# Fused linear attention and SwiGLU kernel: value loads released by the first key, first weight slices 256 columns wide

## The chip, the cores and the metric

One core of one Trainium2 chip runs the whole program. The metric is the device time of one execution in microseconds. Lower is better. Times are medians of several executions on the chip. Every profile is one execution; its span (first to last recorded instruction) is about 2 us shorter than its device time. In this document PE is TensorE, ACT is ScalarE, DVE is VectorE, POOL is GpSimd and SP is the sync engine; POOL and SP issue the DMA loads.

## The reference, cut to what matters

Eight batches, eight heads, 576 tokens, head size 64; then a SwiGLU layer over the 4608 tokens, 512 to 1536 to 512.

```python
q_s = softmax(q, axis=-1)                       # over the head size
k_s = softmax(k, axis=2)                        # over the tokens
kv  = einsum('bhsd,bhse->bhde', k_s, v)
x   = einsum('bhsd,bhde->bhse', q_s, kv)        # then transposed to [tokens, 512]
g   = x @ w_gate
out = (g * sigmoid(g) * (x @ w_val)) @ w_out    # float32
```

## The kernel before

The attention of batch 0 comes first, a chain of short steps that wait for each other. Then PE runs one long stream: the FFN of batch 0 in 12 units (m = 0 to 11, one unit per 128 columns of d_ff), the output products of batch 0 with the attention of batch 1 between them, the FFN of batch 1, and so on.

Queries and keys of batch 0 are loaded by SP. The values of batch 0, and all weights, are loaded by POOL, with DMAs that also cast float32 to bfloat16. POOL issues in program order, so whatever it waits for at the first value load delays every weight behind it:

```python
for G in range(NG):                       # NG = 2 groups of 4 heads
    qd = load("q", q, 0, G)               # SP
    load("k", k, 0, G)
d = nc.gpsimd.dma_start(out=v16[0], in_=head_ap(v, 0, 0))      # POOL, casts
tc.add_manual_dep(d.ins, qd.ins.name, SYNC, reason="order of loads")
for t0, t1 in BANKS:
    nc.gpsimd.dma_start(out=v16[1][:, :, 64*t0:64*t1], in_=head_ap(v, 0, 1, t0, t1))
# ... memsets, exp of q and k, sums ...
for c0, n in ((0, 128), (128, 256), (384, 384), (768, 384), (1152, 384)):
    w_slice(wg, moe_w_gate, c0, n)        # POOL, casts
    w_slice(wv, moe_w_val, c0, n)
w_dma = [wo_slice(m0, 3) for m0 in (0, 3, 6, 9)]
# ... attention of batch 0 ...
load_batch(1, w_dma[-3], by_group=True)   # SP: loads of batch 1 after the 2nd w_out slice
for m in range(MT):
    m_unit(0, S, m, by_part=(m == 0))     # g_ps (wg) and u_ps (wv) of columns 128 m ...
```

After the 12 units come `o_mm(0)`, `o_mm(1)` (output products, o_ps), then the transposes of batch 1's queries (tp), its kv and x products, `o_mm(2)`, `o_mm(3)`, and the FFN of batch 1's first 448 tokens (the g_ps matmuls of 128x448).

The softmax here doesn't subtract the row's maximum and nothing guards it: scores larger than these inputs give would overflow.

Of the kernel before, what the change touches and what calls it, by code (L numbers as in the profile page):

```python
# [11 lines left out]
SYNC = mybir.DependencyInfo(mybir.DependencyClass.Sync, mybir.DependencyReason.DATA)  # L12
# [3 lines left out]
def kernel(  # L16
# [48 lines left out]
    def head_ap(src, b, G, t0=0, t1=T):  # L65
        return bass.AP(
            tensor=src.tensor,
            offset=src[b, 4 * G].offset + 64 * t0,
            ap=[[T * 64, 128], [2 * HSTR, 2], [1, (t1 - t0) * 64]],
        )  # L70

    def load(what, src, b, G, pieces=((0, T),), after=None):
        t_ = ld.tile([128, 2, T * 64], FP32, tag=what, name=what)
        raw[what, b, G] = t_
        last = None
        for t0, t1 in pieces:
            last = nc.sync.dma_start(out=t_[:, :, 64 * t0:64 * t1], in_=head_ap(src, b, G, t0, t1))  # L77
            if after is not None:
                tc.add_manual_dep(last.ins, after.ins.name, SYNC, reason="order of loads")
                after = None  # L80
        return last
# [11 lines left out]
    def w_slice(dst, src, c0, n):  # L93
        ap = bass.AP(
            tensor=src.tensor,
            offset=src[0, c0].offset,
            ap=[[d_ff, 128], [128 * d_ff, KT], [1, n]],
        )
        return nc.gpsimd.dma_start(out=dst[:, :, c0:c0 + n], in_=ap)  # L99
# [251 lines left out]

    make_identity(nc, ident)
    with tc.manual_schedule():
        for G in range(NG):
            qd = load("q", q, 0, G)
            load("k", k, 0, G)
        d = nc.gpsimd.dma_start(out=v16[0], in_=head_ap(v, 0, 0))
        tc.add_manual_dep(d.ins, qd.ins.name, SYNC, reason="order of loads")
        for t0, t1 in BANKS:
            nc.gpsimd.dma_start(out=v16[1][:, :, 64 * t0:64 * t1], in_=head_ap(v, 0, 1, t0, t1))  # L360

# [14 lines left out]
        norm_mul(0, 0, BANKS)  # L376
        norm_sum(0, 1, BANKS)

        for c0, n in ((0, 128), (128, 256), (384, 384), (768, 384), (1152, 384)):
            w_slice(wg, moe_w_gate, c0, n)  # L380
            w_slice(wv, moe_w_val, c0, n)
        w_dma = [wo_slice(m0, 3) for m0 in (0, 3, 6, 9)]
# [199 lines left out]
```

## Time and profile before

| | before |
|---|---|
| device time, median of the first 3 runs | 320.3 us (320.14 to 320.42) |
| span of the profiled run | 318.2 us |
| PE busy | 305.4 us, 96% |
| value load issued by POOL | 8.31 us |
| first kv matmul | 12.45 us |
| first g_ps matmul | 15.81 us |
| first output product (12 FFN units done) | 41.19 us |
| loads of batch 1 start | 35.91 us |

From the page of the kernel before: the span, the busy time of each engine (microseconds, share, number of instructions), and the chain of waits that ended last, by engine and by line.

```profile
span 318.2 us, 4858 instructions
PE 305.4 (96%) x1865; PEld 152.1 (48%) x1894; DVE 163.2 (51%) x277; ACT 147.5 (46%) x218; POOL 29.5 (9%) x37
...
PE 79%; DMA 12%; DVE 3%; POOL 1%; ACT 1%; issue 1%; SPq 1%; DVEq 0%
PE g_ps L298 25%; PE u_ps L298 25%; PE o_ps L322 24%; DMA wo<-in_moe_w_out_dram 5%; DMA q<-in_q_dram 5%; DMA wv<-in_moe_w_val_dram 2%; PE kv L191 2%; DVE rs L138 1%; PE xp L267 1%; DVE qs L152 1%; PE o_ps L342 1%; ACT eq L124 1%; SPq L77 1%
```

PE is busy 96% of the span, but 12% of the chain is DMA. The timeline of the kernel before shows where. Columns: start in us, busy us, engine, line, operation, output<-inputs, shapes, count, and in brackets the idle time before it and what ended it.

```profile
8.04 1.26 ACT L124 ACTIVATE eq<-q 128x640 bf16<-128x640 f32 x2 [0.68 <-DMA q<-in_q_dram]
8.31 0.86 POOL L357 DMA_DIRECT2D v<-in_v_dram  x1 [7.01 <-DMA q<-in_q_dram]
...
12.45 0.68 PE L410 MATMUL kv<-v,ek 64*128 64x128 bf16 x18 [1.08 <-DMA v<-in_v_dram]
...
15.81 0.90 PE L298 MATMUL g_ps<-xt,wg 128*128 128x320 bf16 x4
...
19.15 1.15 PE L298 MATMUL g_ps<-xt,wg 128*128 128x320 bf16 x8 [1.02 <-DMA wg<-in_moe_w_gate_dram]
...
20.60 1.15 PE L298 MATMUL u_ps<-xt,wv 128*128 128x320 bf16 x8 [0.30 <-DMA wv<-in_moe_w_val_dram]
20.84 0.77 POOL L107 DMA_DIRECT2D wo<-in_moe_w_out_dram  x1 [0.71 <-DMA wv<-in_moe_w_val_dram]
...
41.19 5.34 PE L322 MATMUL o_ps<-wo,hr 128*128 128x512 bf16 x23
...
45.82 1.16 ACT L124 ACTIVATE eq<-q 128x1152 bf16<-128x1152 f32 x1 [1.28 <-DMA q<-in_q_dram]
...
46.76 0.68 PE L166 MATMUL tp<-ident,qs 128*128 128x128 bf16 x9 [0.23 <-DVE qs L152]
```

The reader is to see three DMA waits of PE in the first 21 us (1.08, 1.02 and 0.30 us), a value load that POOL issues only when the second query has landed, and a second place that waits for DMA: at 45.82 us ACT starts the exponential of batch 1's second query, 1.28 us after it was free, when that query has landed. The chain of waits in order of time (start, duration, what):

```profile
12.80 7.75 DMA wv<-in_moe_w_val_dram
...
20.84 15.06 DMA wo<-in_moe_w_out_dram
...
37.42 8.37 DMA q<-in_q_dram
...
45.82 1.17 ACT eq L124
```

### The profile page before, as it was taken

The numbers are of one execution on the slowest core, as the hardware profiler recorded it, in microseconds if no ns is written. First come the engines' busy times: TensorE is split into PE (matmuls) and PEld (weight loads), VectorE is DVE, ScalarE is ACT, GpSimd is POOL, SyncE is SP. The second block draws the span as 40 slices with busy tenths as digits, with TensorE's granted clock in tenths as the row PEclk, the third lists the DMA queues.
The fourth block names the chain that finished last, engine by engine and source line by source line (L and its number), as shares of the span: only waits on it lengthen the run. The fifth ranks groups of instructions, "written<-read, shape, count | busy, mean of one in ns | idle before, by whom it ended". The sixth has DMA issues, their size and how long they took to land.

```text
span 318.2 us, 4858 instructions
## 1 busy us (share of the span) xinstructions
PE 305.4 (96%) x1865; PEld 152.1 (48%) x1894; DVE 163.2 (51%) x277; ACT 147.5 (46%) x218; POOL 29.5 (9%) x37
## 2 busy tenths in 40 slices
PE   6789999999999999999999999999999999999994
PEld 2457854454445444544444444444444444444443
DVE  3634467595663558354936393548454333423421
ACT  4653378824654474547374556445734022312300
POOL 0950011200200020002000200020000000000000
PEclk9999999999999999999999999999999999999999
DMA  7999999459164907391539453854320202020124
GB/s 280 134 190 203 239 399 390 158 90 383 61 129 99 387 28 143 70 377 66 118 66 311 158 105 70 270 211 84 69 55 0 55 13 66 0 68 1 33 68 101
DMA packets 40360, 45.75 MB, mean 144 GB/s; under 512 B 17424, under 2 KB 24080, under 8 KB 40336
## 3 DMA queue, kind: packets, MB, share of 16 engines
q1 hardware_dynamic: 32480, 39.99, 41.9%
q0 software_dynamic: 7696, 5.31, 11.5%
q8 instruction: 15, 0.25, 0.3%
q10 hardware_dynamic: 160, 0.13, 0.2%
q14 instruction: 9, 0.07, 0.1%
HBM read 37.75 MB, written 9.44 MB: 148 GB/s over the span
## 4 chain that ended last, share of the span: by engine, by line
PE 79%; DMA 12%; DVE 3%; POOL 1%; ACT 1%; issue 1%; SPq 1%; DVEq 0%
PE g_ps L298 25%; PE u_ps L298 25%; PE o_ps L322 24%; DMA wo<-in_moe_w_out_dram 5%; DMA q<-in_q_dram 5%; DMA wv<-in_moe_w_val_dram 2%; PE kv L191 2%; DVE rs L138 1%; PE xp L267 1%; DVE qs L152 1%; PE o_ps L342 1%; ACT eq L124 1%; SPq L77 1%; POOL wg L99 0%; POOL v L360 0%
## 5 line engine op out<-in xcount | busy, mean ns | idle before, releaser
L305 ACT ACTIVATE sg<-g_ps 128x512 bf16<-128x512 f32 (+2 forms) x120 | 65.0, 554 | 140.2 <-PE g_ps L298 120.6
L306 DVE TENSOR_TENSOR hr<-sg,u_ps 128x512 bf16<-128x512 bf16 (+2 forms) x120 | 74.4, 629 | 88.8 <-PE u_ps L298 81.4
L298 PE MATMUL g_ps<-xt,wg 128*128 128x512 bf16 (+2 forms) x469 | 110.0, 357 | 2.0 <-DMA wg<-in_moe_w_gate_dram 1.0
L298 PE MATMUL u_ps<-xt,wv 128*128 128x512 bf16 (+2 forms) x468 | 109.7, 357 | 0.9 <-DMA wv<-in_moe_w_val_dram 0.3
L322 PE MATMUL o_ps<-wo,hr 128*128 128x512 bf16 x414 | 93.0, 379 | 0.4 <-issue 0.2
L298 PEld LDWEIGHTS <-wv 128*128 128x128 bf16 x480 | 46.9, 98 | 46.9 <-DMA wv<-in_moe_w_val_dram 0.6
L298 PEld LDWEIGHTS <-wg 128*128 128x128 bf16 x480 | 45.7, 98 | 46.5 <-DMA wg<-in_moe_w_gate_dram 1.3
L322 PEld LDWEIGHTS <-hr 128*128 128x128 bf16 x420 | 40.9, 98 | 49.1
L113 DVE COPY o_sb<-o_ps 128x512 f32<-128x512 f32 x33 | 22.4, 680 | 39.2 <-PE o_ps L322 37.3
L127 POOL CAST vb<-v 128x1152 bf16<-128x1152 f32 x14 | 16.0, 1146 | 173.3 <-DMA v<-in_v_dram 173.0
L138 DVE TENSOR_REDUCE rs<-eq 128x18 f32<-128x1152 bf16 (+2 forms) x18 | 21.7, 1214 | 13.1 <-ACT eq L124 13.0
L152 DVE TENSOR_TENSOR qs<-eq,rr 128x1152 bf16<-128x1152 bf16 (+2 forms) x18 | 22.2, 1245 | 0.1
L124 ACT ACTIVATE eq<-q 128x1152 bf16<-128x1152 f32 (+2 forms) x18 | 18.1, 1050 | 4.5 <-DMA q<-in_q_dram 4.5
L124 ACT ACTIVATE ek<-k 128x1152 bf16<-128x1152 f32 x16 | 18.0, 1158 | 0.3 <-DMA k<-in_k_dram 0.2
L305 ACT ACT_TABLE_LOAD x12 | 15.4, 1283 | 0.2
L124 ACT ACT_TABLE_LOAD x11 | 14.1, 1283 | 0.2
L387 PE MATMUL idle<-zero 128*128 128x512 bf16 x20 | 6.5, 480 | 2.8 <-DVE rs L138 1.6
L191 PE MATMUL kv<-vb,ek 64*128 64x129 bf16 x252 | 8.7, 217 | 0.0
L191 PEld LDWEIGHTS <-ek 64*128 64x128 bf16 x252 | 7.3, 94 | 2.7 <-ACT sg L305 2.1
L275 ACT CAST xt<-xp 128x512 bf16<-128x512 f32 x12 | 6.4, 588 | 3.6 <-PE xp L267 3.6
L276 DVE CAST xt<-xp 128x512 bf16<-128x512 f32 x12 | 7.7, 682 | 0.0
L347 ACT COPY o_sb<-o_ps 128x128 f32<-128x128 f32 x2 | 0.5, 265 | 13.3 <-DVE o_sb L346 13.3
(46 smaller groups left out, 72.1 us busy)
## 6 DMA issues: line engine op xcount, KB each, us to landing
q<-in_q_dram SPq DMA_DIRECT2D x16, 576.0 KB, 5.5
k<-in_k_dram SPq DMA_DIRECT2D x16, 576.0 KB, 7.1
out_dram<-o_sb SPq DMA_DIRECT2D x70, 128.0 KB, 2.4
v<-in_v_dram SPq DMA_DIRECT2D x14, 576.0 KB, 8.6
wo<-in_moe_w_out_dram POOLq DMA_DIRECT2D x4, 384.0 KB, 15.1
wg<-in_moe_w_gate_dram POOLq DMA_DIRECT2D x3, 384.0 KB, 11.3
wv<-in_moe_w_val_dram POOLq DMA_DIRECT2D x3, 384.0 KB, 12.5
v<-in_v_dram POOLq DMA_DIRECT2D x1, 288.0 KB, 4.1
```

The costliest lines, as they stand in the source:

```text
L113: eng.tensor_copy(out=out, in_=in_)
L124: nc.scalar.activation(out=e[:, t0:t1], in_=src[:, t0:t1], func=AF.Exp)
L127: nc.gpsimd.tensor_copy(out=vbs[G][:, :, 0:128].rearrange("p t (h d) -> p t h d", d=64), in_=raw["v", b, G].rearrange("p h (t d) -> p t h ...
L138: i = nc.vector.reduce_sum(out=rs[:, 2 * t0:2 * t1], in_=eq2[:, 2 * t0:2 * t1, :], axis=mybir.AxisListType.X)
L152: eng.tensor_mul(qs[:, t0:t1, :].rearrange("p t (h d) -> p (t h) d", d=64), eq2[:, 2 * t0:2 * t1, :], s["rr"][:, 2 * t0:2 * t1].to_broadca ...
L191: nc.tensor.matmul(out=kv[g][:, c:c + 129], lhsT=ek_of(b, G, g, t), rhs=vbs[G][r, t, 0:129], start=(t == 0), stop=(t == T - 1),)
L276: nc.vector.tensor_copy(out=xt[:, 2 * G + 1, c0:c0 + 512], in_=main[G][1])
L298: nc.tensor.matmul(out=gu[a][i][:, 0:w_], lhsT=(wg, wv)[a][:, kk, ms], rhs=xt[:, kk, c:c + w_], start=(kk == 0), stop=(kk == KT - 1),)
L305: nc.scalar.activation(out=sg[:, 0:w_], in_=g_ps[:, 0:w_], func=AF.Silu)
L306: nc.vector.tensor_mul(hr[:, m, r:r + w_], sg[:, 0:w_], u_ps[:, 0:w_])
L322: nc.tensor.matmul(out=o_ps, lhsT=hr[:, m, r0:r0 + 128], rhs=wo[:, m, :], start=(m == 0), stop=(m == MT - 1),)
L387: i = nc.tensor.matmul(out=idle, lhsT=zero[:, 0:128], rhs=zero, start=True, stop=True)
```

## The change

Intent: let POOL start its queue when the first key has landed (about 2 us earlier than the second query), so that values and weights arrive earlier; and give the first weight slices enough columns for two FFN units, with two issues fewer in all.

```diff
+        kd = []
         for G in range(NG):
-            qd = load("q", q, 0, G)
-            load("k", k, 0, G)
+            load("q", q, 0, G)
+            kd.append(load("k", k, 0, G))
         d = nc.gpsimd.dma_start(out=v16[0], in_=head_ap(v, 0, 0))
-        tc.add_manual_dep(d.ins, qd.ins.name, SYNC, reason="order of loads")
+        tc.add_manual_dep(d.ins, kd[0].ins.name, SYNC, reason="order of loads")
 ...
-        for c0, n in ((0, 128), (128, 256), (384, 384), (768, 384), (1152, 384)):
+        for c0, n in ((0, 256), (256, 384), (640, 384), (1024, 512)):
```

## The prediction

> **What bounds the kernel.** TensorE. The page gives PE 305.4 of 318.2 us (96%) and PEclk 9 in every slice, and the stretch table shows PE busy 20.50 of 20.50 us from 20.6 to 41.1 us. What PE lacks lies mostly at the start: 10.7 of the first 15.8 us and 3.46 of 4.80 us between 15.8 and 20.6. So only the first 20 us can gain, and the whole change lives there.
>
> **Waits there (list of waits, timeline).**
> - POOL issues the first value load at 8.31, 0.3 us after the second query landed at 8.01. ScalarE's exponential of the first key starts at 6.20, when that key has landed.
> - PE waits 1.1 us for those values: first kv matmul at 12.45; the key sums before it end at 11.37.
> - PE waits 1.0 us for the second gate slice (g_ps at 19.15) and 0.3 us for the second value slice (u_ps at 20.60).
>
> **What the change moves.** The value load can be issued at about 6.2 + 0.3 = 6.45, so the entire POOL queue of cast loads (values, gate/value slices, w_out) goes 1.85 us earlier. Before, bytes of the value load begin at about 10.0, 1.7 us after issue. In the new kernel that is 8.15; the query and key loads end by 8.3 (DMA share falls from 1.00 to 0.30), so they hardly collide.
>
> **Attention of batch 0.** kv can start when the key sums end, 11.37, instead of 12.45: 1.08 us earlier. Behind it is a chain (the second qs is ready at 11.98), so the first g_ps matmul could start at 14.7 instead of 15.81.
>
> **Weight slices.** The first pair now needs twice the bytes. The DMA view by microsecond: the 128-column slices (256 B packets) move from 13.6 to 15.1 us at 178 GB/s; the 256-column ones (512 B) take from 15.1 to about 18.6, only 103 to 181 GB/s; 384 columns run at 202. The Trainium skill, "DMA: Bandwidth & Descriptors", Specifications, wants 512 B or more for line rate; this trace does not agree that the 256 B packets are the slow ones. So I count no gain from width. Estimate: values done 11.7, then 3.5 us for the first pair: bytes done at 13.5 and 15.2; landing lags bytes by 1 to 2 us in this trace, so the gate slice lands at 14.5 to 15.5, the value slice at 16.2 to 17.2. u_ps of m = 0 waits on it about 1 us (a new wait), m = 1 then none. The value slice for m = 2 lands at about 21.2, wanted at 20.8 to 21.8. Unstalled FFN stream of m = 1 would start at 18.3 to 18.8 rather than 19.6: 0.8 to 1.3 us gained.
>
> **Later.** The batch 1 loads wait for the second w_out slice, landed 35.9; it comes about 1.9 us earlier, so that chain does not eat the gain, and may give 0.2 us more of the 0.8 us PE idle between 41.1 and 56.3.
>
> **Time.** 320.3 - 1.2 = 319.1 us; 8 in 10 within 318.4 to 320.1. Faster by over 2%: 0.005; within 2%: 0.99; slower: 0.005.
>
> **Right if:** first value issue near 6.45; no wait of kv for v; first g_ps near 14.7 to 15.3; a new wait of u_ps on the first wv slice of about 1 us, none at m = 1; w_out's second slice landed near 34.
>
> **Wrong if:** the value loads delay the second query or key (exponentials follow without pause from 8.04, so each delay counts); if the 256-column slices land later than 17.5 us, which returns all; or if they land by 15.3, which makes the gain 1.8 us.

(The 10.7 and 3.46 us in its first paragraph are PE's busy times in those stretches; PE lacks 5.1 and 1.3 us there.)

## The result, and the profile after

317.43 us median (317.24 to 317.75, 4 runs), against 320.22 us (319.5 to 320.42, 4 runs) for the kernel before: 2.8 us less. The ratio is 0.9918, with a 95% interval of 0.99 to 0.9936. A ratio is the mean time of one kernel's fast runs over that of the other's fast runs of the same rounds, so not quite the ratio of the medians quoted. The prediction had 319.1 us and 318.4 to 320.1 us: the direction was right, the class (within 2%) too, but the gain is more than twice the 1.2 us forecast, and the time lies below the range.

The timeline of the changed kernel, the lines that answer to those of before:

```profile
6.36 0.86 POOL L358 DMA_DIRECT2D v<-in_v_dram  x1 [5.05 <-DMA k<-in_k_dram]
...
8.17 1.25 ACT L124 ACTIVATE eq<-q 128x640 bf16<-128x640 f32 x2 [0.93 <-DMA q<-in_q_dram]
...
11.43 0.68 PE L411 MATMUL kv<-v,ek 64*128 64x128 bf16 x18
...
14.87 0.79 PE L298 MATMUL g_ps<-xt,wg 128*128 128x320 bf16 x4
...
16.20 0.72 PE L298 MATMUL u_ps<-xt,wv 128*128 128x320 bf16 x4 [0.54 <-DMA wv<-in_moe_w_val_dram]
16.44 0.78 POOL L107 DMA_DIRECT2D wo<-in_moe_w_out_dram  x1 [0.59 <-DMA wv<-in_moe_w_val_dram]
...
17.63 1.15 PE L298 MATMUL g_ps<-xt,wg 128*128 128x320 bf16 x8
...
20.57 1.15 PE L298 MATMUL u_ps<-xt,wv 128*128 128x320 bf16 x8
```

POOL issues 1.95 us earlier, the second query is hardly later (its exponential starts at 8.17 against 8.04), kv starts 1.02 us earlier. There is a new wait of u_ps for the first value slice (0.54 us), and then none: u_ps of m = 2 starts at 20.57 without one. The chain in order of time now runs through PE almost from 16.2 us on:

```profile
9.38 6.77 DMA wv<-in_moe_w_val_dram
16.20 0.72 PE u_ps L298 x4
...
38.63 0.38 ACT sg L305
...
40.32 1.17 ACT eq L124
...
44.62 0.68 PE tp L166 x9
```

The first output product starts at 39.19 us (41.19 before), the loads of batch 1 at 33.27 (35.91), the exponential of batch 1's second query at 43.63 (45.82), the FFN of batch 1 at 54.14 (56.33). From there to the end both kernels take 261.9 us. So all of the 2.2 us of span in this pair of traces is made before 56 us, 2.0 of it before the first output product. This profiled run was the slowest of the four; over the runs the mean span is 315.68 us.

### The profile page after: what moved, and what is told of

Read it like the earlier page. It is cut to its first block, busy times and chain, and to the rows that moved or that the text cites. A ratio compares the mean times of both kernels' runs of the same rounds, so it can differ in the third digit from the quotient of the medians.

```text
span 316.0 us, 4856 instructions
## 1 busy us (share of the span) xinstructions
PE 304.7 (96%) x1865; PEld 152.0 (48%) x1894; DVE 163.2 (52%) x277; ACT 147.6 (47%) x218; POOL 28.0 (9%) x35
## 4 chain that ended last, share of the span: by engine, by line
PE 88%; DMA 4%; DVE 3%; ACT 2%; issue 1%; POOL 1%; SPq 0%; DVEq 0%
PE g_ps L298 29%; PE u_ps L298 29%; PE o_ps L322 25%; PE kv L191 3%; DMA wv<-in_moe_w_val_dram 2%; DMA k<-in_k_dram 2%; DVE rs L138 1%; PE xp L267 1%; DVE qs L152 1%; PE o_ps L342 1%; ACT L124 1%; ACT eq L124 1%; POOL v L361 0%; PE tp L166 0%; POOL v L358 0%
## 6 DMA issues: line engine op xcount, KB each, us to landing
wo<-in_moe_w_out_dram POOLq DMA_DIRECT2D x4, 384.0 KB, 16.3
wv<-in_moe_w_val_dram POOLq DMA_DIRECT2D x2, 384.0 KB, 10.7
```

## The experiments

Theory T1: the gain is the earlier POOL queue, through PE's waits in the first 20 us; the slices only shift a little. Rival T2: the narrow slices themselves cost about half. Rival T3: what counts is the chain through w_out and the loads of batch 1. All 18 kernels gave correct results. Each call ran the kernel before beside them on the same chip (its mean was 320.0 to 320.6 us in the calls below).

### Each half alone (e1, e2, e3) and a finer grading (e4)

e1: the changed kernel with the old slices.

```diff
-        for c0, n in ((0, 256), (256, 384), (640, 384), (1024, 512)):
+        for c0, n in ((0, 128), (128, 256), (384, 384), (768, 384), (1152, 384)):
```

> New value order with the old slices (128, 256, 384, 384, 384). Theory T1 (the earlier POOL queue alone makes the gain): kv at 11.4, all landings 1.9 us earlier than before, so g_ps of m = 0 at 14.8, second slices landed at 17.2 (gate) and 18.7 (value), the stream of m = 1 unstalled from 17.7: 2.0 to 2.2 us faster than before, like the whole change. Rival T2 (half the gain is the missing narrow slices): 1.0 to 1.3 us faster, with waits at m = 1 of 1 us or more in sum.

e2: the kernel before with the new slices.

```diff
-        for c0, n in ((0, 128), (128, 256), (384, 384), (768, 384), (1152, 384)):
+        for c0, n in ((0, 256), (256, 384), (640, 384), (1024, 512)):
```

> Old value order (second query) with the new slices (256, 384, 384, 512). T1: kv stays at 12.45; first gate slice lands about 16.8, first value slice about 18.1 (6.2 and 6.8 us after issue as in the changed kernel), a wait of u_ps of over 1 us at m = 0, none at m = 1: within 0.4 us of before. T2: about 1 us faster than before.

e3: the changed kernel, no edit.

> The changed kernel again, for the comparison on the same chip: 2.2 to 2.9 us faster than before under every theory.

e4: the changed kernel with slices that start narrow and grow.

```diff
-        for c0, n in ((0, 256), (256, 384), (640, 384), (1024, 512)):
+        for c0, n in ((0, 128), (128, 128), (256, 256), (512, 384), (896, 640)):
```

> New value order with slices 128, 128, 256, 384, 640. T1 with the reading that the changed kernel's PE is held by the first value slice (landed 16.15, wanted 15.5): first value slice lands near 14.3, second pair near 15.7, no wait at m = 0 or m = 1, stream of m = 1 from 17.1 and no later wait over 0.3 us: 0.5 to 0.8 us faster than the changed kernel. T2 (narrow slices are what costs): no faster or slower than the changed kernel.

| run | median us | ratio to before (95%) | mean of runs less mean of before (320.27) |
|---|---|---|---|
| e1 values only | 318.07 | 0.993 (0.9915 to 0.9945) | -2.2 |
| e2 slices only | 319.11 | 0.9968 (0.9953 to 0.9983) | -1.0 |
| e3 whole change | 317.43 | 0.9915 (0.9899 to 0.993) | -2.6 |
| e4 graded | 317.98 | 0.9927 (0.9911 to 0.9942) | -2.3 |

The values alone bring most of it, as T1 said, but the slices alone bring 1.0 us where T1 allowed 0.4, and e4, which was to beat the changed kernel, did not. What I expected of e2 and e4 was wrong.

### Where the loads of batch 1 are moved (e5, e6) and when the values are issued (e7, e8)

e5, on the kernel before, and e6, on the changed kernel:

```diff
-        load_batch(1, w_dma[-3], by_group=True)
+        load_batch(1, w_dma[-4], by_group=True)     # e5: one w_out slice earlier
+        load_batch(1, w_dma[-2], by_group=True)     # e6: one w_out slice later
```

> Kernel before, but the loads of batch 1 wait for the first of the four w_out slices (third before: second), so they start about 2 us earlier; weights and values as before. T1 (the gain is PE's waits of the first 20 us): the first output product still starts at 41.2; only the two pauses of PE before the batch 1 transposes (0.23 and about 0.3 us in the profile of before) can go: 0.2 to 0.5 us faster than before. Rival T3 (the chain of waits through w_out and the batch 1 loads sets the time, its start moved 2 us): 1.5 us or more faster.

> Changed kernel, but the loads of batch 1 wait for the third w_out slice, so they start about 2 us later than in the changed kernel, at about the time of before. T1: loses the part that came after 41 us and a little more, since PE now arrives 2 us earlier at the same loads: slower than the changed kernel by 0.3 to 1.2 us, still 1.4 us or more faster than before. T3: loses the whole gain of 2.6 us, about as slow as before.

e7, on the changed kernel (`kd` now holds the queries):

```diff
-            load("q", q, 0, G)
-            kd.append(load("k", k, 0, G))
+            kd.append(load("q", q, 0, G))
+            load("k", k, 0, G)
```

> Changed kernel, value loads wait for the first query instead of the first key: POOL issues at about 4.9 instead of 6.4. The queries and keys keep the DMA engines full until 8.3, so if more bytes only share them (T1): second query and key land 0.5 to 1.5 us later, kv no earlier than 11.4 and rather at 12 to 12.5, weights land at most 0.3 us earlier: within 0.3 us of the changed kernel or up to 0.8 us slower. If issue time alone counts: another 1 us faster.

e8, on the changed kernel:

```diff
-        tc.add_manual_dep(d.ins, kd[0].ins.name, SYNC, reason="order of loads")
+        tc.add_manual_dep(d.ins, kd[1].ins.name, SYNC, reason="order of loads")
```

> Changed kernel, value loads wait for the second key: POOL issues at about 9.0, later than in the kernel before (8.3). T1: kv at about 13.1 (values land 4.1 us after issue), all weights 2.6 us later than in the changed kernel: 2.0 to 2.8 us slower than the changed kernel, so near the time of before or up to 0.5 us faster than it thanks to the wider slices.

| run | median us | ratio to before (95%) | value load issued |
|---|---|---|---|
| e5 before, loads earlier | 320.29 | 1.0003 (0.998 to 1.0025) | 7.89 |
| e6 changed, loads later | 318.16 | 0.9941 (0.9919 to 0.9962) | 6.42 |
| e7 values after first query | 317.13 | 0.9908 (0.9887 to 0.9929) | 4.79 |
| e8 values after second key | 320.86 | 1.0035 (1.0012 to 1.0057) | 9.75 |

e6 keeps 1.9 of the gain, so T3 in its plain form (the start of the batch 1 loads sets the time) falls. e5 says the same, as slow as before: the loads started at 33.39 instead of 35.91, 2.5 us earlier, but the second query's exponential started at 45.33 instead of 45.82. (About 0.4 us of both leads is not the edit's: in this trace POOL issued its first load at 7.89 instead of 8.31.) Loads that are released into the weight traffic do not land much sooner. e8 is 3.4 us slower than the changed kernel (means 321.12 and 317.68). They were run at other times. POOL issued at 9.75, since the second key landed later than I had assumed, so the size expected (2.0 to 2.8) was missed.

e7 contradicted me. I expected no gain or a loss from colliding loads. The DMA view of e7, by stretch (queue, kind: packets, MB, share of 16 engines; q1 is SP's queue, q0 is POOL's), for 4.8 to 7 us and for 7.8 to 8.0 us:

```profile
q1 hardware_dynamic: 390, 0.83, 102.9%
...
q1 hardware_dynamic: 34, 0.07, 96.3%
q0 software_dynamic: 2, 0.00, 6.6%
```

POOL issued its first load from 4.79 to 5.65 us, yet its first packets come at 7.8 to 8.0, when SP's loads run out. Until then SP's queue has the engines alone, so there was nothing to collide. Here the Trainium skill, "DMA: Bandwidth & Descriptors", Queues, rings and completion order, says that each engine takes turns between the queues that have work, packet by packet; these traces do not show such turns in that stretch. With the engines nearly idle, in the kernel before, POOL's first packets came 1.5 to 1.6 us after the issue began (8.31 to between 9.8 and 9.9); here it took over 3 us. Whether the engines did not take turns, or POOL's descriptors were not ready until then, no run tells.

### Repeats and versions that might be better (e9 to e12)

e9 has the edit of e2, e12 none. e10 and e11 are the changed kernel, and the kernel of e7, with this edit:

```diff
-        for c0, n in ((0, 256), (256, 384), (640, 384), (1024, 512)):
+        for c0, n in ((0, 256), (256, 256), (512, 384), (896, 384), (1280, 256)):
```

> The old value order with the new slices once more, for a second trace: its first trace fell on its slowest run (319.64 of 318.94 to 319.64) and showed the end of the first FFN stretch at 41.21 as before. If the wide slices really give 1 us (theory W: slices of 256 columns and more land sooner after their last bytes than narrow ones), a typical run shows the first output product at 40.4 to 40.9, and the first value slice landed under 1.2 us after the bytes that precede it have moved[...]. If the first trace was typical: 41.2 again.

> Changed kernel with slices 256, 256, 384, 384, 256: the second pair is smaller, so the value slice for m = 2 should land about 1.2 us sooner and the wait of u_ps there (0.44 us in one of the changed kernel's two traces, 0 in the other) go. Theory W: 0.1 to 0.5 us faster than the changed kernel. Rival (number of slices costs): 0.3 us slower or more.

> Value loads issued when the first query has landed (317.13 us with the changed kernel's slices, no wait of PE for weights) and slices 256, 256, 384, 384, 256. Nothing is left for the slices to free: 316.9 to 317.3, within 0.3 us of the version with the changed kernel's slices; candidate for the fastest.

> The changed kernel, as the yardstick of this call: 317.3 to 317.8 us, 0.2 to 0.5 us slower than the version with the first query.

| run | median us | ratio to before (95%) |
|---|---|---|
| e9 slices only (2 runs) | 320.34 | 1.0003 (0.9959 to 1.0048) |
| e10 graded, wide start | 317.82 | 0.9927 (0.9904 to 0.995) |
| e11 e7 with the same slices | 317.72 | 0.9921 (0.9899 to 0.9943) |
| e12 whole change | 317.39 | 0.9914 (0.9893 to 0.9935) |

e9 decides nothing: two runs, 319.38 and 321.3 us, the profiled one with the second query about half a microsecond late (its exponential started at 8.60). e10 and e11 were to be the fastest and are not: ten slice issues instead of eight bought nothing. The rival named for e10 (the number of slices costs 0.3 us or more) fits: e10 is 0.4 us slower than e12 by means.

### The halves again (e13 to e16)

e13 has the edit of e2, e14 that of e1, e15 that of e7, e16 none.

> New slices, old value order, third time. If the wide slices add (theory W): 0.5 to 1.3 us faster than before, and in the trace the value slice that carries columns 128 to 255 lands 1 to 3 us sooner after the second query than in the kernel before. If they only take (the prediction's view): 0.2 us slower to 0.3 us faster.

> Old slices, new value order again: 1.8 to 2.4 us faster than before; theory W: 0.3 to 0.8 us slower than the whole change (e16); the prediction's view: 0.6 us faster than the whole change or more.

> Value loads after the first query, new slices: 0 to 0.4 us faster than the whole change (e16). Its POOL bytes begin with the end of the query and key loads at about 8 us although they are issued at 4.8, and the second query lands within 0.2 us of its time in e16.

> The whole change on the same chip: 2.4 to 2.9 us faster than before.

| run | median us | ratio to before (95%) | mean less mean of before (320.44) |
|---|---|---|---|
| e13 slices only | 318.85 | 0.9956 (0.9932 to 0.9979) | -1.5 |
| e14 values only | 318.39 | 0.9936 (0.9916 to 0.9955) | -2.1 |
| e15 values after first query | 317.32 | 0.9906 (0.9885 to 0.9927) | -3.0 |
| e16 whole change | 317.47 | 0.9908 (0.9889 to 0.9927) | -3.0 |

So the wide slices add to the gain: 1.0 to 1.5 us alone (e2, e13; the two runs of e9 show none), 0.4 to 0.9 us on top of the early values (e1 less e3, e14 less e16, by means). T2 was half right. Issuing after the first query (e15) is the same as the change within 0.1 us; no version here beats the changed kernel clearly.

The puzzle is e14. The lines of its timeline from the first output product on:

```profile
38.42 5.34 PE L322 MATMUL o_ps<-wo,hr 128*128 128x512 bf16 x24
...
44.01 1.16 ACT L124 ACTIVATE eq<-q 128x1152 bf16<-128x1152 f32 x1 [1.85 <-DMA q<-in_q_dram]
...
44.85 0.70 PE L191 MATMUL kv<-vb,ek 64*128 64x129 bf16 x18 [0.32 <-POOL vb L127]
...
49.46 0.68 PE L166 MATMUL tp<-ident,qs 128*128 128x128 bf16 x9 [0.84 <-DVE qs L152]
```

The same lines of the timeline of e16, the whole change on the same chip:

```profile
38.83 5.34 PE L322 MATMUL o_ps<-wo,hr 128*128 128x512 bf16 x24
...
42.86 1.16 ACT L124 ACTIVATE eq<-q 128x1152 bf16<-128x1152 f32 x1 [0.68 <-DMA q<-in_q_dram]
...
44.87 0.70 PE L191 MATMUL kv<-vb,ek 64*128 64x129 bf16 x18
...
48.56 0.68 PE L166 MATMUL tp<-ident,qs 128*128 128x128 bf16 x9
```

With the narrow slices PE ends its first stretch earlier (38.42 against 38.83), and then waits for batch 1: 0.32 us at kv and 0.84 us at the second transposes, because the loads of batch 1 landed later (the second query's exponential starts 1.15 us later). It lost more than it had won. The edit alone did not do this: e1 is the same kernel, and there the second query's exponential came at 43.24. In e14 the first w_out slices landed 2.0 us after POOL's queue had moved as many bytes, in e1 1.2 to 1.5 us (lags are treated below); why, no run shows.

### Is it the lead of the batch 1 loads? (e17, e18)

e17 is e1 and e18 the changed kernel, both with the edit of e5.

> Early values, old slices, batch 1 loads released by the first w_out slice. If the lead of the loads is what the narrow slices lose: loads at 31.5 to 32.5, PE at the first output product still about 38.5, the stretch up to the next FFN product 14.8 to 15.2 us, in all 0.3 to 0.8 us faster than with the second w_out slice (318.1 to 318.4), about like the whole change. If the earlier loads only share the DMA engines with the rest of w_out (as in e5, where the second query landed just 0.5 us earlier for 2.5 us of lead): no gain, 15.2 to 16 us.

> The whole change, batch 1 loads released by the first w_out slice. The stretch is at its floor of 14.8 us already in most traces: within 0.3 us of the whole change (317.4 to 317.7).

e17: 318.3 us, ratio 0.9926 (0.9914 to 0.9938); e18: 317.5 us, ratio 0.9908 (0.9891 to 0.9925). For e17 the second reading holds: the loads started at 31.70 us instead of 33.39 (e1), the second query's exponential at 43.18 instead of 43.24. There is no clear gain over e1 and e14. e18 is as fast as the whole change, as expected. The release of the loads is not what holds them; the weights still in flight are the likely reason, but no run took those away.

### What all traces have in common

Take from each trace O, the start of the first output product, and Q, the start of the exponential of batch 1's second query. Then the second g_ps matmul group of batch 1's FFN starts at the later of O + 14.79 and Q + 10.51, in all 20 traces to within 0.02 us. I found this after the runs, so it is a description, not a forecast that was tested. Its two branches are PE's own work and the landing of the load. Some rows (us, from the timelines):

| trace | first g_ps | O | loads start | Q | O + 14.79 | Q + 10.51 | FFN of batch 1 | span |
|---|---|---|---|---|---|---|---|---|
| before | 15.81 | 41.19 | 35.91 | 45.82 | 55.98 | 56.33 | 56.33 | 318.2 |
| e5 before, loads earlier | 15.33 | 40.48 | 33.39 | 45.33 | 55.27 | 55.84 | 55.84 | 317.7 |
| e2 slices only | 16.33 | 41.21 | 35.34 | 45.19 | 56.00 | 55.70 | 56.01 | 317.9 |
| e13 slices only | 15.77 | 40.25 | 34.47 | 44.42 | 55.04 | 54.93 | 55.04 | 316.9 |
| e1 values only | 14.49 | 38.55 | 33.39 | 43.24 | 53.34 | 53.75 | 53.77 | 315.9 |
| e14 values only | 14.71 | 38.42 | 34.16 | 44.01 | 53.21 | 54.52 | 54.52 | 316.4 |
| changed | 14.87 | 39.19 | 33.27 | 43.63 | 53.98 | 54.14 | 54.14 | 316.0 |
| e12 changed | 15.07 | 39.05 | 33.18 | 43.02 | 53.84 | 53.53 | 53.84 | 315.7 |
| e16 changed | 14.95 | 38.83 | 32.64 | 42.86 | 53.62 | 53.37 | 53.62 | 315.5 |
| e6 changed, loads later | 14.80 | 39.12 | 35.38 | 44.23 | 53.91 | 54.74 | 54.73 | 316.6 |
| e7 values after first query | 14.63 | 38.38 | 32.50 | 42.47 | 53.17 | 52.98 | 53.18 | 315.0 |

The kernel before is held by Q, by 0.35 us over O in its one trace. The values alone move O by 2.6 to 2.8 us but Q by only 1.8 to 2.6, so Q holds them and part of PE's gain is lost. With the wide slices on top O comes 0.3 to 1.2 us later (39.62 in e3 is the largest), while Q (42.86 to 43.63) is not clearly earlier than with narrow ones (43.18 to 44.01). The FFN of batch 1 starts at 53.62 to 54.41 with wide slices and at 53.68 to 54.52 with narrow ones, so these traces do not show where the wide slices' share on top of the early values arises. The mean spans of all runs do show one: 0.2, 0.6 and 0.3 us less (e3 less e1, e16 less e14, e18 less e17). So T1 holds for most of the gain, T2 for a part of it, and T3 is true of one branch: the landing of batch 1's query, not the release of its load.

One difference between traces is not an edit's, for the same kernel shows both forms. In seven of the 20 (e3, e5, e8, e12, e13, e16, e18) PE's six warm-up matmuls before the first key sums take 2.74 us instead of 1.47, one every 0.43 us instead of 0.21, and the key sums start at 8.7 to 8.9 instead of 7.4 to 7.7. Three of the four traces of the changed kernel are among them and none of e1, e14 and e17, so part of the difference in O may be this. No run shows what decides it.

Two more facts belong to the sum. First, the device time less the span is 1.78 to 1.84 us on average in every kernel with eight weight-slice issues, and 1.97 to 2.14 us in every one with ten (before: 2.01 to 2.10). So about 0.25 us of the change lies outside the profiled span. It explains most of what e10 loses to e12: e10's mean time is 0.4 us longer while its mean span (315.80) is within 0.13 us of e12's (315.67). It is also 0.2 to 0.3 us of the 0.4 to 0.9 us that the wide slices add. Why it is so no run shows.

Second, the landing. I take the value slice that brings column 255, which the second FFN unit (m = 1) needs. In POOL's queue everything up to it is 1.11 MB with the wide slices (values 0.59 MB, one pair of 256 columns 0.52 MB), but 1.38 MB with the narrow ones, where that slice holds columns 128 to 383 (two pairs, 0.79 MB). By the DMA view the queue has moved that much by the time in the fourth column; the slice landed at the time in the second, which is the issue of the w_out slice that waits for it (the POOL lines of w_out shown above) less 0.3 us, the delay seen at POOL's other releases (second query 8.01, POOL 8.31). A w_out slice waits for a weight slice because in all these traces POOL issues a DMA only after the one eight issues before it has landed: the second w_out slice is the 15th issue in the kernel before and the 13th in the changed one, and waits for the 7th and the 5th.

| trace | slice landed | MB up to it | moved by | lag |
|---|---|---|---|---|
| before (narrow) | 20.54 | 1.38 | 18.6 | 1.9 |
| e1, e14, e17 (narrow) | 17.90, 17.56, 17.31 | 1.38 | 16.6, 16.5, 16.5 | 1.3, 1.1, 0.8 |
| changed, e3, e12, e16 (wide) | 16.14, 15.96, 15.55, 15.78 | 1.11 | 15.3, 15.0, 14.6, 14.6 | 0.8 to 1.2 |
| e2, e13 (wide) | 17.60, 17.06 | 1.11 | 16.8, 16.3 | 0.8 each |

The DMA view of the kernel before, POOL's queue alone (packets, MB, share), from 8 to 18.6 us and from 8 to 20.5 us:

```profile
q0 software_dynamic: 2879, 1.37, 109.8%
...
q0 software_dynamic: 3412, 1.74, 113.2%
```

The same of the changed kernel from 5 to 15.3 us and from 5 to 16.1 us:

```profile
q0 software_dynamic: 1843, 1.11, 81.8%
...
q0 software_dynamic: 2082, 1.28, 85.6%
```

So that slice landed 4.4 to 5.0 us earlier than before, and the table splits it. About 2.0 us are the earlier queue (1.38 MB at 16.5 instead of 18.6). About 1.4 us are the smaller first pair: 0.26 MB less has to move before that slice is complete, and e1, e14 and e17 take 1.4 us from 1.11 MB (15.1 us) to 1.38 MB. The rest is a shorter lag (0.8 to 1.2 us instead of 1.9), and in e12 and e16 bytes that had moved 0.5 us sooner than in e1. PE does not turn all of this into gain: with early values and narrow slices u_ps of m = 1 waits 0.17 us in e1 and not at all in e14 and e17, so on top of the early values the smaller pair frees nothing there. It helps where the values are late (e2, e13).

These traces do not tie the lag to the width. (My theory W, in the expectations of e9, e10, e13 and e14, rested on a lag of 3.3 us in the kernel before. That figure, cut from e9's expectation, was a wrong count: it took 1.11 MB there too, but those end with the gate slice.) With the early queue the narrow slices lag 0.8 to 1.3 us and the wide ones 0.8 to 1.2. In the kernel before, the two 128-column slices landed 0.9 to 1.0 us after their bytes and the two 256-column ones behind them 1.9; and in the changed kernel the second gate slice, 384 columns wide, lagged 1.5, 2.2, 2.3 and 1.2 us in the four traces. While a slice is on its way to landing the queue moves bytes of the next ones: 0.36 MB of 1.74 in the kernel before, 0.17 of 1.28 in the changed one. Whether packets overtake each other or the landing is only reported late, and what sets the lag, no run shows.

## Why the prediction was wrong

- **What bounds the kernel, the POOL queue, the attention.** Right. POOL was predicted at 6.45 and issued at 6.36; POOL's bytes at 8.15 and first seen between 8.0 and 8.2; no real delay of the second query; kv at 11.37 and found at 11.43 (11.68 to 12.01 in the three other traces, those with the slow warm-up; kv waited for no values there either); the first g_ps at 14.7 to 15.3 and found at 14.87 (14.95 to 15.28 in the three other traces).
- **The step that failed: "landing lags bytes by 1 to 2 us in this trace, so the gate slice lands at 14.5 to 15.5, the value slice at 16.2 to 17.2".** The bytes of the value slice were about right (15.2 predicted, 14.6 to 15.3 found), in the first trace by luck: the values were done at 12.3 instead of 11.7, and the first pair took 3.0 us instead of 3.5. The gate slice was right too (landed about 14.8 in the first trace). The lag of the value slice was mis-sized. The stream start of 18.3 to 18.8, less the 1.6 us that the rest of m = 0 took before, corresponds to a landing at 16.7 to 17.2, so to a lag of 1.5 to 2.0 us, which is what the 256-column slices show in the trace before (1.9); the 128-column slices of the same trace lag 0.9 to 1.0. Found were 0.8 to 1.2 us, so the value slice landed at 15.55 to 16.14, ahead of the whole predicted range. The "new wait of about 1 us" is 0.54 us in one trace of the changed kernel and absent in the three others.
- **The value slice for m = 2, "at about 21.2".** It landed at 20.4, 20.9, 20.4 and 19.8 us in the four traces (the issue of the last w_out slice less 0.3 us): its bytes had moved by 18.6 to 19.3, and it lagged 1.1 to 1.9 us.
- **Therefore the FFN stream.** Predicted to gain 0.8 to 1.3 us; O gained 2.0 us in the first trace and 1.6 to 2.4 over the four. The mechanism was right and this term was mis-sized by the landings: with the measured 16.15 in place of 16.7 and no wait at m = 2, the prediction's own steps give 16.15 + 1.6 = 17.75 for the stream of m = 1 (u_ps of m = 0 to its end took 1.6 us before), 1.9 us before 19.6. The ceiling of 1.8 us that I set was too low as well: with the values alone O gained 2.6 to 2.8 us, because the slice that PE waited for landed 2.6 to 3.2 us earlier (20.54 to 17.9, 17.56 and 17.31) for 1.9 us of earlier issue: 2.0 to 2.1 us of it in the bytes, the rest in a lag that was 1.9 us in the trace before and 0.8 to 1.3 in these.
- **"So only the first 20 us can gain."** Wrong as a reading of the profile. The chain of waits, quoted above, showed the kernel before held by the load of batch 1, not by PE, while PE's own work would have been ready 0.35 us sooner. I used it only as a remark. (The release of those loads hangs on POOL's queue, so the edits of the first 20 us moved them too.) The forecast that this chain "does not eat the gain" and may give 0.2 us more came out: the stretch from O to the FFN of batch 1 took 15.14 us before, 14.95 in the first trace after, 14.79 in the others.
- **Not seen at all:** 0.25 us outside the span, with two issues fewer.
- **The skill's line-rate rule.** The prediction held against the Trainium skill, "DMA: Bandwidth & Descriptors", Specifications (512 B or more for line rate), that the 256 B packets moved at 178 GB/s. That was true of the mean rate, and the landings do not contradict it: the 128-column slices lagged least (0.9 to 1.0 us). "So I count no gain from width" was wrong all the same. With the values late, the wide slices gain 1.0 to 1.5 us (e2, e13): 0.26 MB less, 1.4 us of the queue, has to move until column 255 is complete. On top of the early values they gain 0.4 to 0.9 us, 0.2 to 0.3 of it outside the span; where the rest arises is open.

The sum over the four traces of the changed kernel, against the one trace of the kernel before: O gains 2.0 us on average, the stretch behind it 0.3, outside the span 0.25, in all about 2.6 us, where the means of the runs give 2.6 to 3.0. The prediction had 0.8 to 1.3, 0.2 and nothing.

## What to carry to other kernels

When a queue of loads is issued in program order, the wait on its first entry is paid by everything behind it: release it by the earliest transfer that still keeps the engines full. Cost a slice by how many bytes stand in the queue up to the last column that is wanted, and add the lag to its landing; take that lag from several traces and slices, for here it ran from 0.7 to 2.3 us and one trace gave the wrong one. Where two chains meet soon after the stretch you are improving, write down both times: once one of them has moved by the distance between them, only the other one pays.

## What the Trainium skill lacked or had wrong

- "DMA: Bandwidth & Descriptors", Anatomy of one DMA, gives a fixed cost of about 2.0 us, most of it after the last byte, as about constant. Measured from the time that the queue had moved as many bytes, the gate and value slices here landed 0.7 to 2.3 us later, and the same slice of the same kernel 1.2 to 2.3 us (the second gate slice of the changed kernel in four traces).
- The same page, Queues, rings and completion order, has each engine take turns between queues with work. With POOL's load issued at 4.79 us, SP's queue kept the engines until 7.8 us (390 packets to none from 4.8 to 7 us). Whether POOL had work ready for them before that is not shown.
- The same page, Specifications, gives about 1 us to the first byte for POOL's DMAs. In the kernel before, with the engines nearly idle, POOL's issue began at 8.31 us and ended at 9.17, and its first four packets were seen between 9.8 and 9.9: 1.5 to 1.6 us from the beginning, 0.6 to 0.7 from the end.
- No page has it: two fewer weight-load issues shortened the device time outside the profiled span by about 0.25 us (1.78 to 1.84 against 1.97 to 2.14).
